# All attention heads as float32 products on row and column halves of TensorE, with w_val and w_out kept in SBUF

## The chip, the cores and the metric

The kernel runs on one core of a Trainium2 chip. The core has TensorE (matrix products, PE in the profile), VectorE (DVE), ScalarE (ACT), GpSimd (POOL) and SyncE (SP), which work through their own queues in the order in which the program lists them, and 16 DMA engines that move data between HBM and SBUF. The metric is the time of one execution in microseconds (us); less is better.

## The reference

Three stages follow each other on float32 data: batch 4, 12 heads, 448 tokens, head size 64, so a model width of 768.

```python
def _attn_ref(q, k, v):
    scores = scale * np.matmul(q, k.transpose(0, 1, 3, 2)) - np.log(S)
    attn = 1.0 / (1.0 + np.exp(-scores))
    return np.matmul(attn, v)
...
def _moe_ref(x, w_val, conv_w, w_out):
    for k in range(K):                       # K = 5, causal, per channel
        gate_pre += conv_w[k][None, None, :] * xp[:, k:k + S, :]
    gate = 1.0 / (1.0 + np.exp(-gate_pre))
    val = x @ w_val
    return (gate * val @ w_out)
...
def _moe2_ref(x, w_tok1, w_tok2, w_ch1, w_ch2):
    h = np.maximum(xt @ w_tok1, 0.0) @ w_tok2
    u = x + h.transpose(0, 2, 1)
    h2 = np.maximum(u @ w_ch1, 0.0) @ w_ch2
    return (u + h2)
```

The weights arrive as float64, which the kernel reads as pairs of 32-bit words; q, k and v are float32.

## The kernel before, in words

**Number formats.** Nearly every product is made of float32r parts. A float32 value x is split into H (x rounded to 12 significant bits) and L = x - H; a product is then three passes (H by H, L by H, H by L), each one PE instruction of 448 columns. A weight is decoded on the chip: `decode` takes a raw tile of float64 words, `[128, 2*768]` int32, and makes H and L with six DVE operations (lines 97, 99, 100, 103, 107 and 108) and two ACT operations (98 and 106). Raw tiles have two buffers, so the load of a piece waits until the piece two before it is decoded to the end (line 108).

**Attention.** The 12 heads of a batch are taken as 6 pairs (24 pairs in all). `KINDS` says how a pair is multiplied. Pairs 0 to 7 are kind n: float32 products on full tiles for the scores (`scores`, line 269; k is padded with zeros so that the 128 rows of one head's k and zeros meet both heads' q), and for attention times values (`native_av`) one full product (line 334) and then 3 products into each column half of TensorE (line 338), first the three of one head, then the three of the other. Pair 8 has split scores and float32 values. Pairs 9 to 23 are kind x: 16 float32r products for the scores (line 275) and 14 for the values (line 322), for which ACT computes every sigmoid twice (line 258, one into float32, one into H) and DVE takes the differences (lines 296, 299, 300) and splits q, k and v.

**Dense layers.** `post_pair` turns the attention output of a pair into H and L (`xs`) and into a gate by a convolution (line 353, four DVE operations). `dense_steps(b)` lists the products of batch b: w_val (108 instructions), w_out (108), transposes, w_tok1, w_tok2; both w layers are line 395. The list is woven between the attention pairs of batch b + 1 by `weave`; the last batch's list runs alone. Decoded w_val and w_out are written to HBM (`wscr`, line 175) and read back per column group and per batch (`w_load`, line 366, 42 loads), except that batch 0 uses w_val where it was decoded.

**Channel layers.** For each batch and each of 12 groups `fc` of 128 hidden channels, `ch1` (line 593) and `ch2` (line 607) make 18 products each. The 12 pairs of weight pieces are decoded once (`dec_ch`), the first `CHAN_LEFT` = 5 of them into a pool that becomes free when attention ends, the other 7 into a pool that takes the place of the dense layers' tiles and must wait for them.

**Order.** The queue of each engine is fixed when the program is built, by a scheduler that follows data dependences and priorities. A queue does not overtake itself: what stands behind a waiting instruction on DVE, ACT or SP waits too.

Of the kernel before, what the change touches and what calls it, by code (L numbers as in the profile page):

```python
# [24 lines left out]


@with_exitstack
def tile_kernel(ctx, tc, qT, kT, v, w_val, conv_w, w_out, w_tok1, w_tok2, w_ch1, w_ch2, out):
    """Every float32 product is made of float32r parts: x = H + L with H = x rounded to 12
    significant bits and L = x - H, which has 12 as well, so H and L are exact operands of a  # L30
    single-pass matmul. The weights come as float64 words and are split on chip into the same
    two parts. Activations are kept feature-major ([feature, token]). The attention of batch b + 1
    runs beside the dense layers of batch b; the first pairs of heads, when the weights are still
    being split, are multiplied as float32 instead."""
    nc = tc.nc
# [19 lines left out]
    KIND = KINDS + "x" * (NPT - len(KINDS))  # L55
# [4 lines left out]
    wscr = dram.tile([2, KD, P, 2, KD, P], F32, name="wscr")  # L60
# [23 lines left out]
    # --- float64 words -> float32 parts. The high word's sign, exponent (rebased by 896) and top  # L84
    # 11 fraction bits make hi; the other 9 + 32 fraction bits, times 2^(exponent - 20), make lo.
# [41 lines left out]
    wv = {}  # L127

    def dec_conv(pool):
        n = KD * KW  # L130

        def go(raw):
            st = pool.tile([P, 2, DM], F32R, tag="st", bufs=1, name="cwHL")
            h, lo = st[:, 0, :n], st[:, 1, :n]
# [22 lines left out]
    def dec_w(pool, sel, kk):  # L157
        w = (w_val, w_out)[sel]

        def go(raw):  # L160
            if sel == 0 and kk >= 2:
                tag = VAL_TAGS[kk - 2]
                hl = [attn.tile([P, DM], F32R, tag=tag, bufs=2, name=f"wv{n}") for n in range(2)]
            else:
                if sel == 0:
                    st = wts.tile([P, 2, DM], F32R, tag="wst", bufs=3, name="wv")
                else:
                    st = pool.tile([P, 2, DM], F32R, tag="st", bufs=1, name="st")
                hl = [st[:, n] for n in range(2)]
            if sel == 0:  # L170
                wv[kk] = hl
# [12 lines left out]
        return ld, go  # L184

    # ------------------------------------------------------------------ attention
    raw_t, hl_t, a_t = {}, {}, {}
    x_t, xs_t, gate_t = {}, {}, {}

    def load_qk(i):  # L190
# [508 lines left out]
```

## Time and profile before

| | |
|---|---|
| median of 3 runs | 817.37 us (816.83 to 820.62) |
| span of the profiled execution | 821.3 us, 0.5% above that median; the page gives no other time of this execution |
| PE matmul | busy 795.0 us, 97% of the span, 3712 instructions |
| PE weight loads | 677.8 us, 83% |
| DVE | 499.5 us, 61% |
| ACT | 389.4 us, 47% |
| DMA | 119.79 MB, mean 146 GB/s |

The busy time of PE is the sum of overlapping matmuls, so 97% is not a measure of how well PE works; the starts of its instructions are. A float32r product of 448 columns and a float32 product of 448 columns are not the same work: the profile counts two PE instructions for one float32 product. The page cuts the span into 40 slices of 20.5 us.

### The profile page before, as it was taken

What the parts mean: (1) busy time and instruction counts of PE and PEld (TensorE: products, weight loads), DVE (VectorE), ACT (ScalarE), POOL (GpSimd) and SP (SyncE); (2) the same over time, 40 slices, a digit from 0 to 9 for tenths busy, and PEclk for the clock granted to TensorE, in tenths of its full rate; (3) what the DMA queues carried; (4) which work ended last, traced back from release to release, by engine and by line L of the source; (5) the groups of instructions that cost most, each with busy time, mean ns of one, the idle gap of its engine ahead of it and who ended that gap; (6) DMA issues with size and microseconds to landing.
All of it is one profiled execution on the core that took longest, in us unless ns stands there. A gap on an engine that the chain in (4) does not pass through costs nothing.

```text
span 821.3 us, 10042 instructions
## 1 busy us (share of the span) xinstructions
PE 795.0 (97%) x3712; PEld 677.8 (83%) x3712; DVE 499.5 (61%) x818; ACT 389.4 (47%) x564; POOL 24.1 (3%) x83
## 2 busy tenths in 40 slices
PE   8899899999999999999998999999999999999998
PEld 3333487789998899988887899999999999999997
DVE  5877587789978899797768999962002200030002
ACT  6575465889788888897334444430002100020000
POOL 3221110000000000000000000000000000000000
PEclk9999989999999999999999999999999999999999
DMA  7898767564774547523687455424001400050001
GB/s 236 259 275 251 199 199 232 172 192 121 238 224 144 171 139 215 194 78 111 228 329 236 154 186 184 160 94 146 1 1 40 162 1 1 1 166 24 1 1 67
DMA packets 77855, 119.79 MB, mean 146 GB/s; under 512 B 7648, under 2 KB 68976, under 8 KB 77808
## 3 DMA queue, kind: packets, MB, share of 16 engines
q1 hardware_dynamic: 75984, 110.09, 42.5%
q0 software_dynamic: 1824, 9.08, 3.4%
q8 instruction: 29, 0.48, 0.2%
q14 instruction: 18, 0.15, 0.1%
HBM read 98.70 MB, written 20.45 MB: 145 GB/s over the span
## 4 chain that ended last, share of the span: by engine, by line
PE 77%; DMA 8%; DVE 6%; issue 5%; ACT 2%; POOL 1%; SPq 0%; POOLq 0%; DVEq 0%; ACTq 0%
PE psh L593 21%; PE pso L607 21%; PE psd L395 17%; PE pss L275 5%; PE psy L322 4%; PE pst L449 3%; DMA wscr<-st 3%; PE pst L436 3%; DMA raw<-w_tok 2%; DVE acc L353 1%; DMA raw<-w_ch 1%; DMA raw<-w_val 1%; PE pst L419 1%; DMA raw<-w_out 1%; DVE st L108 1%
## 5 line engine op out<-in xcount | busy, mean ns | idle before, releaser
L607 PE MATMUL pso<-r,wch 128*128 128x448 f32 x864 | 185.2, 366 | 0.0
L593 PE MATMUL psh<-us,wch 128*128 128x448 f32 x864 | 183.7, 366 | 0.0
L593 PEld LDWEIGHTS psh<-us,wch 128*128 128x128 f32 x864 | 162.3, 188 | 13.8
L607 PEld LDWEIGHTS pso<-r,wch 128*128 128x128 f32 x864 | 162.1, 188 | 13.7
L78 DVE SCALAR_TENSOR_TENSOR r<-psh,r 128x448 fp32r<-128x448 f32 x48 | 29.9, 623 | 215.7 <-ACT r L76 215.6
L76 ACT ACTIVATE r<-psh 128x448 fp32r<-128x448 f32 x48 | 26.0, 543 | 232.3 <-PE psh L593 232.0
L395 PE MATMUL psd<-gv,wst 128*128 128x448 f32 x432 | 98.0, 373 | 2.5 <-ACT x2T L410 2.4
L395 PEld LDWEIGHTS psd<-gv,wst 128*128 128x128 f32 x432 | 81.7, 191 | 11.3 <-ACT x2T L410 3.5
L395 PE MATMUL psd<-xs,wst 128*128 128x448 f32 x324 | 70.1, 366 | 0.0
L353 DVE SCALAR_TENSOR_TENSOR acc<-x,cw,acc 128x448 f32<-128x448 f32 x96 | 65.3, 681 | 0.8
L258 ACT ACTIVATE a<-pss,bias_s 128x896 f32<-128x896 f32 x60 | 60.4, 1007 | 10.2 <-PE pss L275 8.9
L395 PEld LDWEIGHTS psd<-xs,wst 128*128 128x128 f32 x324 | 60.9, 188 | 5.0
L98 ACT ACTIVATE dec_a<-dec_a,exp_b 128x768 int32<-128x768 int32 (+3 forms) x43 | 37.4, 869 | 53.9 <-DVE dec_a L97 51.3
L258 ACT ACTIVATE aH<-pss,bias_s 128x896 fp32r<-128x896 f32 x60 | 60.4, 1007 | 0.0
L269 PE MATMUL pss<-qn,kn 128*128 128x448 f32 x112 | 48.9, 578 | 11.5 <-POOL ident masks.py:199 4.0
L269 PEld LDWEIGHTS pss<-qn,kn 128*128 128x128 f32 x112 | 20.7, 198 | 36.9 <-issue 21.4
L275 PE MATMUL pss<-qH,kHL 128*128 128x448 f32 x128 | 47.5, 371 | 0.1
L275 PE MATMUL pss<-qL,kHL 128*128 128x448 f32 x128 | 46.7, 365 | 0.0
L322 PE MATMUL psy<-aH,vHL 128*128 128x448 f32 x120 | 39.3, 368 | 0.0
L103 DVE SCALAR_TENSOR_TENSOR dec_a<-raw,dec_a 128x768 int32<-128x768 int32 (+2 forms) x42 | 37.2, 887 | 3.2 <-ACT dec_a L98 3.1
L258 ACT ACTIVATE an<-pss,bias_s 128x896 f32<-128x896 f32 (+2 forms) x38 | 33.0, 881 | 10.9 <-PE pss L269 10.5
L100 DVE SCALAR_TENSOR_TENSOR dec_c<-raw,dec_c 128x768 f32<-128x768 uint32 (+2 forms) x42 | 37.3, 889 | 0.8
(93 smaller groups left out, 997.9 us busy)
## 6 DMA issues: line engine op xcount, KB each, us to landing
wst<-wscr SPq DMA_DIRECT2D x42, 768.0 KB, 4.7
raw<-w_ch SPq DMA_DIRECT2D x24, 768.0 KB, 4.4
rq<-qT SPq DMA_DIRECT2D x32, 224.0 KB, 4.7
rk<-kT SPq DMA_DIRECT2D x32, 224.0 KB, 3.8
uscr<-x2T SPq DMA_DIRECT2D x24, 224.0 KB, 3.0
u<-uscr SPq DMA_DIRECT2D x24, 224.0 KB, 4.2
ur<-uscr SPq DMA_DIRECT2D x24, 224.0 KB, 3.3
out<-ur SPq DMA_DIRECT2D x24, 224.0 KB, 2.2
```

Source lines behind the costliest of these rows:

```text
L78: nc.vector.scalar_tensor_tensor(out=l_out, in0=src, scalar=0.0, in1=f(h_out), op0=ALU.max, op1=ALU.subtract)
L98: nc.scalar.activation(out=a, in_=a, func=AF.Relu, scale=8.0, bias=exp_b)
L100: nc.vector.scalar_tensor_tensor(out=c.bitcast(F32), in0=lo.bitcast(U32), scalar=2.0**-32, in1=c, op0=ALU.mult, op1=ALU.add)
L103: nc.vector.scalar_tensor_tensor(out=a, in0=hi, scalar=-0x80000000, in1=a, op0=ALU.bitwise_and, op1=ALU.bitwise_or)
L258: nc.scalar.activation(out=out, in_=ps, func=AF.Sigmoid, bias=bias_s[rows], scale=QK_SCALE)
L269: nc.tensor.matmul(ps[:, cc, :S], k[:, at : at + P], q, start=True, stop=True)
L275: nc.tensor.matmul(ps[:, cc, :S], kHL[:, j, c * P : (c + 1) * P], mv[:, j, :], start=n == 0, stop=n == 1)
L322: nc.tensor.matmul(y[:, :S], lhsT, m, start=n == 0, stop=n == len(mv) - 1)
L353: nc.vector.scalar_tensor_tensor(out=acc, in0=x[:, t : t + S], scalar=cw[:, p * KW + t : p * KW + t + 1], in1=acc, op0=ALU.mult, op1=ALU.add,)
L395: nc.tensor.matmul(ps[:, :S], w(a, kk), s[:, c, :], start=kk == 0 and n == 0, stop=kk == KD - 1 and n == 2,)
L593: nc.tensor.matmul(ps[:, :S], wch[fc][:, 0, a, kk * P : (kk + 1) * P], us_t[b, kk][:, c, :], start=kk == 0 and n == 0, stop=kk == KD - 1 a ...
L607: nc.tensor.matmul(acc[j][:, :S], wch[fc][:, 1, a, j * P : (j + 1) * P], r[:, c, :], start=fc == 0 and n == 0, stop=fc == KF - 1 and n == 2,)
```

## The change

All 24 pairs are multiplied as float32. A score product now takes the 64 rows of one head: head 0 on rows 0 to 63 of TensorE, head 1 on rows 64 to 127, each into its own PSUM bank, 8 products in a pair. A value product takes all 128 rows and 64 columns: head 0 in columns 0 to 63, head 1 in columns 64 to 127, alternating, 8 products in a pair. There is one sigmoid for both heads of a chunk of 128 keys, and no split of q, k, v or of the attention weights. Decoded w_val lives in a pool `wval` on the left until the last batch has used it, decoded w_out in `wts`; `wscr`, its stores and its loads are gone. The pool for the first channel weights is opened only after w_val is released, and holds 3 groups in place of 5. `DEC_AT` says how many weight pieces are decoded beside each pair.

```diff
-KINDS = "nnnnnnnns"
-VAL_TAGS = ("qH", "qL", "kHL", "vHL")
-CHAN_LEFT = 5
+CHAN_LEFT = 3
+A_BUFS = 4
...
+DEC_AT = (1, 2, 2, 2, 2, 2, 2, 1, 1, 1, 1, 1)
...
-    wscr = dram.tile([2, KD, P, 2, KD, P], F32, name="wscr")
...
+    wval = tc.alloc_tile_pool(name="wval", bufs=1, side="left")
     attn = tc.alloc_tile_pool(name="attn", bufs=1, side="left")
...
+    wres = [
+        [[pool.tile([P, DM], F32R, name=f"w{sel}_{kk}_{n}") for n in range(2)] for kk in range(KD)]
+        for sel, pool in enumerate((wval, wts))
+    ]
...
-            decode(pool, DM, raw, hl[0], hl[1])
-            with tc.high_priority(0 if sel else -10):
-                for n in range(2):
-                    nc.sync.dma_start(
-                        wscr[sel, :, :, n, kk, :].rearrange("j p m -> p j m"),
-                        f(hl[n][:]).rearrange("p (j m) -> p j m", m=P),
-                    )
...
-        return ld, go
+        return ld, lambda raw: decode(pool, DM, raw, *wres[sel][kk])
...
+    def load_pair(i):
+        b, p = divmod(i, NP)
+        h0 = 2 * p
+        q = attn.tile([P, S], F32, tag="q", bufs=2, name="q")
+        k = attn.tile([P, S], F32, tag="k", bufs=2, name="k")
+        t = attn.tile([P, NF + 1, P], F32, tag="v", bufs=2, name="v")
+        nc.sync.dma_start(q, qT[b, h0 : h0 + 2].rearrange("h d s -> (h d) s"))
+        nc.sync.dma_start(k, kT[b, h0 : h0 + 2].rearrange("h d s -> (h d) s"))
...
+    def scores(i, c):
+        q, k, _ = raw_t[i]
         ps = psa.tile([P, 2, 512], F32, tag="s", bufs=2, name="pss")
+        at = KLAST if c == NF else c * P
+        for j in range(2):
+            rows = slice(j * D, (j + 1) * D)
+            nc.tensor.matmul(ps[:, j, :S], k[rows, at : at + P], q[rows], start=True, stop=True)
+        a = attn.tile([P, 2, S], F32, tag="a", bufs=A_BUFS, name="a")
+        nc.scalar.activation(out=a, in_=ps[:, :, :S], func=AF.Sigmoid, bias=bias_s, scale=QK_SCALE)
+        a_t[i, c] = a
+
+    def av(i):
+        vn = raw_t.pop(i)[2]
         y = psa.tile([P, 512], F32, tag="y", bufs=2, name="psy")
+        for c in range(NF + 1):
+            a = a_t.pop((i, c))
+            for j in range(2):
                 cols = slice(j * D, (j + 1) * D)
+                nc.tensor.matmul(y[cols, :S], vn[:, c, cols], a[:, j], start=c == 0, stop=c == NF)
+        x = attn.tile([P, PAD + S], F32, tag="x", bufs=2, name="x")
+        nc.gpsimd.memset(x[:, :PAD], 0.0)
+        nc.scalar.activation(out=x[:, PAD:], in_=y[:, :S], func=AF.Copy)
+        x_t[i] = x
...
-    def w_load(b, sel, j):
-        st = wts.tile([P, 2, KD, P], F32R, tag="wst", bufs=3, name="wst")
-        nc.sync.dma_start(f(st[:]), wscr[sel, j])
-        w_t[b, sel, j] = st
...
-                if held:
-                    return wv[kk][a][:, j * P : (j + 1) * P]
-                return w_t[b, sel, j][:, a, kk, :]
+                return wres[sel][kk][a][:, j * P : (j + 1) * P]
...
+        av(i)
+        if i + 1 < NPT:
+            scores(i + 1, 0)
+            scores(i + 1, 1)
+        if i + 2 < NPT:
+            load_pair(i + 2)
+        for _ in range(DEC_AT[i] if i < len(DEC_AT) else 0):
+            dec_go()
+        weave((base + 0.5) / NP * fast)
+        if i + 1 < NPT:
+            scores(i + 1, 2)
+            scores(i + 1, 3)
+        post_pair(i)
+        weave((base + 1.0) / NP * fast)
...
-    pso = tc.alloc_tile_pool(name="pso", bufs=1, space=bass.MemoryType.PSUM)
-    left = tc.alloc_tile_pool(name="p2l", bufs=1, side="left")
-    dec2 = tc.alloc_tile_pool(name="dec2", bufs=1, side="left")
...
     for fn in [fn for n, fn in tail] + rest[:nval]:
         fn()
+    wval.release()
+    pso = tc.alloc_tile_pool(name="pso", bufs=1, space=bass.MemoryType.PSUM)
+    left = tc.alloc_tile_pool(name="p2l", bufs=1, side="left")
+    dec2 = tc.alloc_tile_pool(name="dec2", bufs=1, side="left")
```

The change also moves instructions in the queues. On PE, beside the dense layers of batch 0, the queue before holds only full-tile products (line 395 dense, 322 values, 275 scores):

```order
L395 MATMUL psd<-gv,wst 128x448 x6
L322 MATMUL psy<-aL_1289,vHL 128x448
L322 MATMUL psy<-aH,vHL 128x448
L322 MATMUL psy<-aL_1313,vHL 128x448
L322 MATMUL psy<-aH,vHL 128x448
L395 MATMUL psd<-gv,wst 128x448 x6
L275 MATMUL pss<-qH,kHL 128x448
L275 MATMUL pss<-qL,kHL 128x448
L275 MATMUL pss<-qH,kHL 128x448
L275 MATMUL pss<-qL,kHL 128x448
L395 MATMUL psd<-gv,wst 128x448 x6
```

Of the change, at about the same place in the program (line 206 values on column halves, 194 scores on row halves, 267, 284 and 297 dense layers on full tiles):

```order
L267 MATMUL pst<-ident,x2T 128x128 x4
L206 MATMUL psy<-a,v 64x448
L297 MATMUL pst_1318<-wt2H,h_1149 128x448 x2
L297 MATMUL pst_1318<-wt2L,h_1149 128x448
L297 MATMUL pst_1318<-wt2H,h_1164 128x448 x2
L297 MATMUL pst_1318<-wt2L,h_1164 128x448
L267 MATMUL pst<-ident,x2T 128x128 x4
L206 MATMUL psy<-a,v 64x448 x7
L194 MATMUL pss<-q,k 128x448 x4
L284 MATMUL pst_1365<-x_1210,wt1H 128x384
```

PE now goes from one form of product to another (full tile, column halves, row halves) five times in these rows; in the whole queue it does so 121 times, against 28 times before, and 95 of the 121 come behind the first column group of w_out of batch 0.

On DVE, at the start of the program, where the first dense products are read out of PSUM (line 405 `gate`, then `gv`), the queue before has the gates of w_val ahead of most of the w_tok1 pieces (128x256):

```order
L97 TENSOR_SCALAR dec_a<-raw 128x256
L108 SCALAR_TENSOR_TENSOR st<-dec_c,raw 128x768
L405 TENSOR_TENSOR gate<-psd,gate 128x448
L99 TENSOR_SCALAR dec_c<-raw 128x256
L103 SCALAR_TENSOR_TENSOR dec_a<-raw,dec_a 128x256
L100 SCALAR_TENSOR_TENSOR dec_c<-raw,dec_c 128x256
L405 TENSOR_TENSOR gate<-psd,gate 128x448
L107 TENSOR_SCALAR raw<-dec_a 128x256
L82 TENSOR_TENSOR gv<-gate,gv 128x448
```

In the change the last three gates of w_val (line 253) stand behind the last w_tok1 piece and among the two w_tok2 pieces (128x448); these are the fourth and the fifth:

```order
L108 SCALAR_TENSOR_TENSOR wt1L<-dec_c,raw 128x256
L253 TENSOR_TENSOR gate<-psd,gate 128x448
L97 TENSOR_SCALAR dec_a<-raw 128x448
L99 TENSOR_SCALAR dec_c<-raw 128x448
L82 TENSOR_TENSOR gv<-gate,gv 128x448
L100 SCALAR_TENSOR_TENSOR dec_c<-raw,dec_c 128x448
L103 SCALAR_TENSOR_TENSOR dec_a<-raw,dec_a 128x448
L107 TENSOR_SCALAR raw<-dec_a 128x448
L97 TENSOR_SCALAR dec_a<-raw 128x448
L108 SCALAR_TENSOR_TENSOR wt2L<-dec_c,raw 128x448
L253 TENSOR_TENSOR gate<-psd,gate 128x448
```

So the reading of the last w_val groups now follows the loads of the last weight pieces.

On DVE again, where the dense layers of the last batch end (the last three `x2T` are line 453 before) and the channel layers begin, the queue before has its ninth channel piece finished (line 108) ahead of the last three `x2T`:

```order
L108 SCALAR_TENSOR_TENSOR wch<-dec_c,raw 128x768
L453 TENSOR_TENSOR x2T<-pst_4397,x2T 128x448
L99 TENSOR_SCALAR dec_c<-raw 128x768
L453 TENSOR_TENSOR x2T<-pst_4406,x2T 128x448
L100 SCALAR_TENSOR_TENSOR dec_c<-raw,dec_c 128x768
L453 TENSOR_TENSOR x2T<-pst_4415,x2T 128x448
```

In the change (line 301) it is the seventh piece that comes behind the last `x2T`:

```order
L301 TENSOR_TENSOR x2T<-pst_3433,x2T 128x448
L301 TENSOR_TENSOR x2T<-pst_3442,x2T 128x448
L301 TENSOR_TENSOR x2T<-pst_3451,x2T 128x448
L108 SCALAR_TENSOR_TENSOR wch<-dec_c,raw 128x768
L99 TENSOR_SCALAR dec_c<-raw 128x768
L78 SCALAR_TENSOR_TENSOR r<-psh,r 128x448
L100 SCALAR_TENSOR_TENSOR dec_c<-raw,dec_c 128x768
```

Where 9 of the 24 channel pieces were finished at this point, 6 are now.

## Rows read from the trace of the kernel before

**Rows 1.** The page, part 2: busy tenths of each engine in 40 slices.

```profile
PE   8899899999999999999998999999999999999998
...
DVE  5877587789978899797768999962002200030002
```

**Rows 2.** Busy time by stretch: us, PE, PEld, DVE, ACT, POOL, PEclk, DMA share, GB/s.

```profile
9.40:47.40 38.00, 34.05 (x99) 14.95 (x98) 31.94 (x46) 25.16 (x34) 6.58 (x18) 1.00 0.91 269
47.40:104.00 56.60, 49.85 (x139) 21.36 (x137) 37.17 (x59) 31.91 (x46) 7.84 (x22) 0.96 0.80 231
250.00:300.00 50.00, 49.19 (x252) 44.19 (x251) 45.17 (x74) 44.22 (x64) 0.30 (x3) 1.00 0.47 144
450.00:500.00 50.00, 50.00 (x249) 44.66 (x248) 47.90 (x76) 21.89 (x30) 0.00 (x0) 1.00 0.53 175
```

**Rows 3.** Timeline of PE: start, us to the last end, line, tile, form, count.

```profile
21.24 3.28 PE L338 MATMUL psy<-an,rv 128*64 128x448 f32 x12
24.45 2.40 PE L395 MATMUL psd<-xs,wv 128*128 128x448 f32 x10
...
64.78 2.47 PE L338 MATMUL psy<-an,rv 128*64 128x448 f32 x6
67.18 1.77 PE L269 MATMUL pss<-qn,kn 128*128 128x448 f32 x4
...
74.63 3.27 PE L269 MATMUL pss<-qn,kn 128*128 128x448 f32 x8
77.83 2.47 PE L338 MATMUL psy<-an,rv 128*64 128x448 f32 x6
...
88.96 3.17 PE L269 MATMUL pss<-qn,kn 128*128 128x448 f32 x8
91.96 0.92 PE L334 MATMUL psy<-an,rv 128*128 128x448 f32 x2
...
121.52 5.11 PE L395 MATMUL psd<-gv,wst 128*128 128x448 f32 x24
...
396.64 22.19 PE L395 MATMUL psd<-xs,wst 128*128 128x448 f32 x108
418.68 7.59 PE L395 MATMUL psd<-gv,wst 128*128 128x448 f32 x36
```

**Rows 4.** Line 108 up to 140 us: its tiles, durations, starts, and who waited.

```profile
L108 DVE SCALAR_TENSOR_TENSOR wv<-dec_c,raw x6: 947/958/960, 14.7 to 46.5; 128x768 fp32r<-128x768 f32 x6
L108 DVE SCALAR_TENSOR_TENSOR st<-dec_c,raw x6: 951/959/993, 58.6 to 102.9; 128x768 fp32r<-128x768 f32 x6
...
L108 DVE SCALAR_TENSOR_TENSOR wt1L<-dec_c,raw x4: 416/416/419, 106.5 to 122.3; 128x256 fp32r<-128x256 f32 x4
L108 DVE SCALAR_TENSOR_TENSOR wt2L<-dec_c,raw x2: 624/625/626, 131.8 to 134.4; 128x448 fp32r<-128x448 f32 x2
...
  DMA wscr<-st: 5.6, 2
```

**Rows 5.** Groups on DVE: busy us, mean ns, idle time before, what ended it.

```profile
L353 DVE SCALAR_TENSOR_TENSOR acc<-x,cw,acc 128x448 f32<-128x448 f32 x96 | 65.3, 681 | 0.8
...
L405 DVE TENSOR_TENSOR gate<-psd,gate 128x448 f32<-128x448 f32 x24 | 14.9, 620 | 1.2 <-PE psd L395 0.9
```

**Rows 6.** Timeline, DVE and PE, where the last channel pieces are decoded and used.

```profile
472.60 7.59 PE L593 MATMUL psh<-us,wch 128*128 128x448 f32 x36
...
534.00 0.55 DVE L97 TENSOR_SCALAR dec_a<-raw 128x768 int32<-128x768 int32 x1
...
537.51 0.96 DVE L108 SCALAR_TENSOR_TENSOR wch<-dec_c,raw 128x768 fp32r<-128x768 f32 x1
538.39 0.55 DVE L97 TENSOR_SCALAR dec_a<-raw 128x768 int32<-128x768 int32 x1
...
542.71 3.84 PE L593 MATMUL psh<-us,wch 128*128 128x448 f32 x18
```

**Rows 7.** DMA issues: engine, count, KB each, median us to landing.

```profile
raw<-w_val POOLq DMA_DIRECT2D x3, 768.0 KB, 7.3
```

More of the change, by code (lines that the diff above doesn't have):

```diff
@@ L54, in tile_kernel @@
     NPT = B * NP
[L55 removed]
+    KLAST = S - P
     assert D == 64 and REM == 64 and NF == 3
@@ L132, in go @@
         def go(raw):
-            st = pool.tile([P, 2, DM], F32R, tag="st", bufs=1, name="cwHL")
-            h, lo = st[:, 0, :n], st[:, 1, :n]
+            h = attn.tile([P, n], F32R, tag="acc", bufs=2, name="cwH")
+            lo = attn.tile([P, n], F32R, tag="acc", bufs=2, name="cwL")
             decode(pool, n, raw, h, lo)
@@ L202, in load_v @@
-    def load_v(i, diag):
-        b, p = divmod(i, NP)
-        t = attn.tile([P, NF + 1, 2 * D], F32, tag="rawv", bufs=2, name="rv")
-        vs = v[b, :, 2 * p * D : 2 * (p + 1) * D]
-        nc.sync.dma_start(t[:, :NF], vs[:R0].rearrange("(c p) x -> p c x", p=P))
-        for r in range(2):
-            rows, cols = slice(r * REM, (r + 1) * REM), slice(r * D, (r + 1) * D)
-            if diag:
-                nc.gpsimd.memset(t[rows, NF, (1 - r) * D : (2 - r) * D], 0.0)
-                nc.sync.dma_start(t[rows, NF, cols], vs[R0:, cols])
-            else:
-                nc.sync.dma_start(t[rows, NF], vs[R0:])
-        return t
@@ L330, in native_av @@
-    def native_av(i):
-        vn = raw_t.pop(i)[2]
-        a = [[a_t.pop((i, j, part)) for part in range(2)] for j in range(2)]
-        y = psa.tile([P, 512], F32, tag="y", bufs=2, name="psy")
-        nc.tensor.matmul(y[:, :S], vn[:, NF], a[0][1][:, 1], start=True, stop=False)
-        for j in range(2):
-            for c in range(NF):
-                cols = slice(j * D, (j + 1) * D)
-                nc.tensor.matmul(
-                    y[cols, :S], vn[:, c, cols], a[j][c // 2][:, c % 2], start=False, stop=c == NF - 1
-                )
-        nc.scalar.activation(out=new_x(i)[:, PAD:], in_=y[:, :S], func=AF.Copy)
+        nc.sync.dma_start(k, kT[b, h0 : h0 + 2].rearrange("h d s -> (h d) s"))
@@ L359, in post_pair @@
         gate_t[i] = gate
-    w_t = {}
-    def w_load(b, sel, j):
-        st = wts.tile([P, 2, KD, P], F32R, tag="wst", bufs=3, name="wst")
-        nc.sync.dma_start(f(st[:]), wscr[sel, j])
-        w_t[b, sel, j] = st
     def dense_steps(b):
-        units = [(b, sel, j) for sel in range(1 if b == 0 else 0, 2) for j in range(KD)]
         gv, x2T, x2, h1 = {}, {}, {}, {}
@@ L374, in proj @@
         def proj(sel, j, part):
-            held = b == 0 and sel == 0
             if part == 0:
-                u = -1 if held else units.index((b, sel, j))
-                if u == 0:
-                    for k in units[:2]:
-                        if k not in w_t:
-                            w_load(*k)
-                if not held and u + 2 < len(units):
-                    w_load(*units[u + 2])
                 cur["ps"] = psd.tile([P, 512], F32, tag="d", bufs=2, name="psd")
@@ L400, in proj @@
                 return
-            if not held:
-                del w_t[b, sel, j]
             if sel == 0:
@@ L483, in tile_kernel, with dec_load @@
     raws = []
-    def dec_load(first=False):
+    def dec_load():
         if decs:
             ld, go = decs.pop(0)
-            if first:
-                raw = wts.tile([P, 2 * DC], I32, tag="wst", bufs=3, name="raw")
-                ld(raw)
-            else:
-                raw = fetch(dec, ld)
-            raws.append((raw, go))
+            raws.append((fetch(dec, ld), go))
     def dec_go():
@@ L501, in tile_kernel @@
     load_pair(0)
-    dec_load(True)
     dec_load()
-    prep_pair(0)
-    craw = attn.tile([P, 2 * KD * KW], I32, tag="tmp", bufs=3, name="craw")
+    load_pair(1)
+    dec_load()
+    craw = attn.tile([P, 2 * KD * KW], I32, tag="craw", bufs=1, name="craw")
     ld, go = dec_conv(dec)
@@ L524, in late @@
         dn["late"] = tc.alloc_tile_pool(name="late", bufs=1, side="right")
-    scores(0, 0)
-    scores(0, 1)
-    for g in range(NH):
-        b, base = divmod(g, HB)
+    for c in range(NF + 1):
+        scores(0, c)
+    for i in range(NPT):
+        b, base = divmod(i, NP)
         fast = 0.95 if b == B - 1 else 1.0
@@ L537, in tile_kernel @@
             emitted = 0
-        if g % 2 == 0 and g // 2 + 1 < NPT:
-            load_pair(g // 2 + 1)
-            prep_pair(g // 2 + 1)
-        dec_go()
-        if g + 1 < NH:
-            scores(g + 1, 0)
-        weave((base + 0.33) / HB * fast)
-        if g + 1 < NH:
-            scores(g + 1, 1)
-        weave((base + 0.67) / HB * fast)
-        av(g)
-        if g % 2 == 1:
-            post_pair(g // 2)
-        weave((base + 1.0) / HB * fast)
+        av(i)
[12 more added lines that the diff above has]
+        weave((base + 1.0) / NP * fast)
     tail = pend
```

138 lines of the change are left out of this document (7 added, 131 removed).

## The prediction

> **What bounds the kernel now.** I read the slices of the page first. TensorE (PE) is at 80 or 90% and more in every slice, while VectorE (DVE) falls from the eighties and nineties to almost nothing over the last third [rows 1]. The stretches say the same with numbers: PE is busy 49.19 of 50 us from 250 and 50.00 of 50 from 450, but only 34.05 of 38 and 49.85 of 56.6 in the first 104 us [rows 2]. So PE bounds the middle and the end, and something else has a say at the start. Since busy time on PE is a sum of overlapping records, I took prices from starts in the timeline [rows 3]: 108 float32r products start within 418.68 - 396.64 = 22.04 us, so one costs 0.204 us. Eight float32 records take 91.96 - 88.96 = 3.00 us, so one costs 0.375 and a float32 product, which is two records, 0.75.
>
> DVE at the start does the decoding. One piece of 768 columns takes 538.39 - 534.00 = 4.39 us from the first operation to the first of the next [rows 6]. Line 108, its last operation, is 0.96 us there, 0.416 for w_tok1 and 0.625 for w_tok2 [rows 4], so I scale those pieces to 1.9 and 2.86 us.
>
> **What column halves and changes of form cost.** Three products into each column half, 12 records, take 24.45 - 21.24 = 3.21 us where 12 records in a row would take 4.5: the halves do run at once [rows 3]. The six records of one head alone take 67.18 - 64.78 = 2.40, which is 0.15 over 6 x 0.375. Eight score records followed by another form take 77.83 - 74.63 = 3.20, which is 0.20 over 3.00 [rows 3]. So going from one form to another costs 0.15 to 0.20 us, and it adds to the product time. I take 0.15 for the 21 changes into column halves and 0.20 for the other 74 behind the first column group of w_out; going into row halves stands in no row, and 0.20 is the nearer of the two since it, too, exposes a weight load. The bounds are 0 and 0.20.
>
> **The price of a pair.** A pair of kind x is 30 x 0.204 = 6.1 us now. After the change, 8 score products on row halves and 8 value products on column halves cost 8 x 0.375 = 3.0 each if both halves run at once: 6.0 us. No product on 64 rows stands in this trace. The column halves are the nearest row and overlap, so I take full overlap; the bounds are none (6.0 for the scores) and full (3.0).
>
> **Term A, the start.** I cut the program where the first column group of w_out of batch 0 ends: now at 121.52 + 18 x 0.204 = 125.2 us [rows 3], with the values of pair 7 still to do. The changed queue reaches the same place with the values of pair 7 and half of the scores of pair 8 done. PE has some 79 us of products and changes up to there (8 pairs at 6.5 with their changes, half a pair's scores 1.5, 108 x 0.204 = 22 and 18 x 0.204 = 3.7), so I asked DVE. It has 12 pieces x 4.39 = 52.7, four of w_tok1 7.6, two of w_tok2 5.7 (the gates of the last w_val groups now stand behind these), and 12 gates or `gv` at 0.62 less 0.08 overlap [rows 5] 6.4. The 0.08 is what line 108 overlaps the next decode: 0.96 long, 0.88 to the next start [rows 6]. Eight `post_pair` have four convolution operations of 0.681 each [rows 5], 0.60 by the same overlap, and one subtraction like a gate, 2.94 in all, so 23.5. The sum is 95.9 us from 9.4. If DVE never waited the cut would come at 105. It was busy 31.94 of 38 us in the first stretch, 84%, and 37.17 of 56.6, 66%, in the second [rows 2]. The waits of the second stretch include those on the `wscr` stores of `st`, 5.6 us in the row of line 108 [rows 4], which the change removes. What remains is the loads: a raw tile takes 7.3 us from issue to landing on POOL's queue [rows 7] against 4.39 of decoding, with two buffers. I take 90%: 9.4 + 95.9/0.9 = 116, so A = -9. The bounds are 100% (-20) and 84% (-2).
>
> **Term B, attention behind the cut.** Before: the values of pair 7 at 0.75 + 3.2 = 4.0, pair 8 with 16 x 0.204 = 3.3 and again 4.0, and 15 pairs at 6.1 = 91.8, together 103.1. After: half of the scores and the values of pair 8, 4.5, and 15 x 6.0 = 90, together 94.5; and the changes of form, 21 x 0.15 + 74 x 0.20 = 17.9, so 112.4. B = +9.3. What the change saves on products (8.6 us) is less than what it pays for the changes, because the dense products woven between are on full tiles. The bounds are -8.6 with changes that cost nothing, and those of the rivals below.
>
> **Term C, the channel layers.** When the dense layers of the last batch end (472.60 is the first double `ch1` [rows 6]), 9 of the 24 weight pieces are decoded now; afterwards 6 are, because the pool waits for w_val and holds three groups, and the rest for the dense tiles. Three decodes are 13.2 us. DVE has nearly no slack there, 47.90 of 50 us [rows 2]. The last piece is now ready at 538.39 and its products start at 542.71 [rows 6], so 4.3 us of the 13.2 are covered and 8.9 are not: PE would wait for `wch` in the last groups of batch 0. C = +9. It is 13 or 14 if what covers is gone, and 3 if DVE, with less work ahead, begins sooner or needs less than its share of a group.
>
> **Term D, waits in the middle.** PE is idle 0.81 of 50 us with DVE at 90% and ACT at 88% [rows 2], some 4.5 us over 275. The differences and second sigmoids go, so I take half back: D = -2 (0 to -4).
>
> **At nothing.** The stores and loads of `wscr` and the new long-lived tiles: the DMA engines were 47% busy in the middle [rows 2] and PE did not wait for loads there. In the first 47 us their share is 0.91, and that is in A. The new score loads are smaller than the old ones.
>
> **Sum.** 821.3 - 9 + 9.3 + 9 - 2 = 828.6 us of span. The median is 817.37 for a profiled span of 821.3, a factor 0.9952: 824 us. A difference under 0.5%, 813.3 to 821.5, is one that the measurement can't tell from no change.
>
> **The rivals.**
>
> *Changes of form are hidden* (faster). If the next form's weights load while the last product of the old form still streams, the 17.9 us are not paid, B is -8.6 and the span 810.7: 807 us. Against it stand the 2.40 and 3.20 us [rows 3], but they come from places with one change each, and none into row halves. It decides when a change costs less than 0.07 us: 95 x (0.19 - 0.07) = 11 us turn 824 into 813. At half price it is 815. TensorEngine Tiling (Array Packing) of the Trainium skill, section Key Properties, says that a change of tiling mode drains TensorE, which speaks against this rival; the trace agrees with 0.15 and 0.20 us.
>
> *DVE never waits at the start.* With no stores to wait for, loads could keep ahead. A is -20 rather than -9: 813.5, and 809 with the lower end of C. For it: 5.6 us of the waits are gone. Against it: two raw buffers, and 7.3 us to a load. It holds from a DVE share of 95% on.
>
> *Row halves overlap only in part.* If each of four chunks in a pair exposes one weight load, at the 0.20 us of a change into full form, 15.5 pairs cost 12.4 us more: 841 of span, 837 us. TensorE: Matmul & The Clock Gate of the Trainium skill, Part 3, measured 3.07 times for four row tiles, not four; by that ratio scores would cost 1.3 times 3.0, an estimate of +14 us and 838. No run here shows it yet.
>
> *Row halves do not overlap at all*, so that the change doesn't do what it says. Scores cost 6.0, 15.5 x 3.0 = 46.5 us more behind the cut, and nothing at the start, where 79 + 24 us of PE still fit under DVE's 107: 875 of span, 871 us. For it speaks only that no row has 64-row products; against it that the column halves overlap.
>
> **How the numbers follow.** The forecast as summed has 0.48, with 811 to 837 as its own range from the ends of A, C and D. Hidden changes have 0.18, DVE without waits 0.16, partial overlap 0.10 and none 0.08. The range 806 to 839 leaves out the last and the tails of the others. Faster: 0.15 from hidden changes, 0.07 from the start, 0.03 from my own range, 0.25. Same: 0.12 of my own, 0.09 of the start, 0.03 of changes at half price, 0.24. Slower: 0.33 of my own, 0.10 and 0.08 of the two overlap cases, 0.51.
>
> **What the profile after would show.** Eight score records of two heads starting in 1.5 us, in pairs at nearly one time, or in 3.0 if rows do not overlap. Between the last record of one form and the first of another, 0.15 to 0.20 us over 0.375 or 0.204. The first w_out group of batch 0 starting at about 112 us, with DVE at some 90% until then. `ch1` of the last groups of batch 0 waiting on DVE for `wch`, 9 us in all. In the middle, PE without idle time but for the changes. The forecast is wrong if the changes cost under 0.07 us, if DVE's share at the start is near 100% or near 80%, or if `ch1` never waits.

## The result and the profile after

The change makes the kernel slower: 827.61 us median (824.15 to 829.17) against 817.37, a ratio of 1.0105 with a 95% interval of 1.0075 to 1.0135. The profiled execution has a span of 827.1 us against 821.3. Executions in which the granted clock fell for a long time are left out of every ratio, and the profile of e4 below (clock 0.656, 1099.4 us) is one of them, so its stages are not known. I cut both traces at the two places where the prediction cut its sum: the end of the first column group of w_out of batch 0, and the start of the last product of the dense layers of the last batch.

| us from the trace | before | after | difference | predicted |
|---|---|---|---|---|
| start, up to the cut | 125.2 | 112.7 | -12.5 | A -9 |
| from the cut to the end of the dense layers | 347.2 | 357.3 | +10.1 | B +9.3, D -2 |
| channel layers and the end | 348.9 | 357.1 | +8.2 | C +9 |
| span | 821.3 | 827.1 | +5.8 | +7.3 |

Of the first 18 products of `ch2`, all lie before the second place in the kernel before and 13 in the change. So 1.0 us of products moved across it: like for like the middle is 11.1 us longer and the channel layers 7.2.

The slices of VectorE on the page show where work went. They answer to [rows 1]:

```profile
DVE  5898844243433434234589399993002200030002
```

After the first slice VectorE is still at eight and nine tenths up to 100 us, falls to two to four tenths through the middle, and is full in slices 24 to 27, where the channel pieces are decoded. The busy times by stretch answer to [rows 2] (us, PE, PEld, DVE, ACT, POOL, granted clock, DMA share, GB/s):

```profile
9.40:47.40 38.00, 29.63 (x123) 9.45 (x121) 35.37 (x54) 30.69 (x41) 6.05 (x12) 0.91 0.57 198
47.40:104.00 56.60, 50.62 (x215) 28.10 (x217) 50.19 (x94) 38.84 (x57) 8.21 (x18) 0.91 0.47 150
...
250.00:300.00 50.00, 48.72 (x234) 31.98 (x235) 20.09 (x35) 20.48 (x31) 0.90 (x6) 1.00 0.19 60
```

From 9.4 to 104 VectorE is busy (35.37 + 50.19) / 94.6 = 90% of the time. From 250 to 300 its load has more than halved, from 45.17 to 20.09 us, and TensorE is no busier for it: 48.72 where it was 49.19 [rows 2].

The timeline of TensorE from the cut on (line 194 is scores on row halves, 206 values on column halves, 245, 284 and 297 dense, 267 transposes; the last four rows, with `ch1` in line 431 and `ch2` in 445, are from the channel layers) answers to [rows 3]:

```profile
108.45 5.66 PE L245 MATMUL psd<-gv,w 128*128 128x448 f32 x24
...
149.91 3.23 PE L206 MATMUL psy<-a,v 128*64 128x448 f32 x16
153.07 1.77 PE L194 MATMUL pss<-q,k 64*128 64x448 f32 x8
154.78 0.67 PE L297 MATMUL pst<-wt2H,h 128*128 128x448 f32 x2
...
161.12 1.77 PE L194 MATMUL pss<-q,k 64*128 64x448 f32 x8
162.82 1.49 PE L245 MATMUL psd<-gv,w 128*128 128x448 f32 x6
164.15 0.60 PE L267 MATMUL pst<-ident,x2T 128*128 128x128 f32 x4
164.68 0.97 PE L206 MATMUL psy<-a,v 128*64 128x448 f32 x2
165.57 0.67 PE L297 MATMUL pst<-wt2H,h 128*128 128x448 f32 x2
...
166.89 0.60 PE L267 MATMUL pst<-ident,x2T 128*128 128x128 f32 x4
167.42 3.22 PE L206 MATMUL psy<-a,v 128*64 128x448 f32 x14
170.57 1.77 PE L194 MATMUL pss<-q,k 64*128 64x448 f32 x8
172.28 0.44 PE L284 MATMUL pst<-x,wt1H 128*128 128x384 f32 x1
...
181.56 0.36 PE L297 MATMUL pst<-wt2L,h 128*128 128x448 f32 x1
181.85 3.23 PE L206 MATMUL psy<-a,v 128*64 128x448 f32 x16
185.00 1.77 PE L194 MATMUL pss<-q,k 64*128 64x448 f32 x8
...
512.58 0.47 PE L431 MATMUL psh<-us,wch 128*128 128x448 f32 x1 [0.59 <-ACT wch L106]
...
541.49 0.47 PE L431 MATMUL psh<-us,wch 128*128 128x448 f32 x1 [0.41 <-ACT wch L106]
542.20 3.72 PE L431 MATMUL psh<-us,wch 128*128 128x448 f32 x17 [0.24 <-DVE wch L108]
546.55 3.93 PE L445 MATMUL pso<-r,wch 128*128 128x448 f32 x18 [0.63 <-ACT r L76]
```

Three things stand in the rows up to 185 us. Eight score records of two heads take 162.82 - 161.12 = 1.70 us: 1.50 for four in a row in each half, both halves at once, and 0.20 for the change of form. Sixteen value records take 185.00 - 181.85 = 3.15, which is 3.00 and 0.15. And where the scheduler put the first value product of a pair alone (164.68, the products of the other seven at 167.42), it has no partner in the other half: 0.89 us for two records, and the fourteen still take 3.15, so the pair pays 0.89 more than in one piece. Four of the 16 pairs behind the cut are split like this, one of them into three.

The table of waits (us in all, times, longest us), in this order: TensorE from the cut to 470 us, TensorE in the channel layers of batch 0 (470 to 560), VectorE up to 115 us:

```profile
PE pst L284 <- ACT x L269: 2.7, 3, 1.3
PE psd L245 <- ACT x2T L258: 2.2, 2, 2.0
PE psd L245 <- DVE x2T L301: 1.0, 1, 1.0
...
PE psh L431 <- ACT wch L106: 1.7, 4, 0.6
PE pso L445 <- ACT r L76: 1.3, 2, 0.6
PE psh L431 <- DVE wch L108: 0.7, 2, 0.4
...
DVE dec_a L97 <- DMA raw<-w_val: 5.4, 3, 3.0
DVE dec_a L97 <- DMA craw<-conv_w: 4.8, 1, 4.8
DVE dec_a L97 <- DMA raw<-w_tok: 3.6, 3, 2.1
DVE dec_a L97 <- DMA raw<-w_out: 2.2, 2, 1.5
```

In the middle TensorE waits for copies of transposes and for the reading of PSUM. In the same channel layers the kernel before has no wait on TensorE at all; here decoding comes late piece after piece (the last four rows of the timeline), which costs by many small waits, not by one long one. At the start VectorE waits for almost nothing but raw weights.

### The profile page after: what moved, and what is told of

The parts are those of the page before. It is cut to its first block, busy times and chain, and to the rows that moved or that the text cites. A ratio compares the mean times of both kernels' runs of the same rounds, so it can differ in the third digit from the quotient of the medians.

```text
span 827.1 us, 9458 instructions
## 1 busy us (share of the span) xinstructions
PE 793.3 (96%) x3776; PEld 612.5 (74%) x3776; DVE 376.0 (45%) x635; ACT 295.7 (36%) x440; POOL 20.7 (2%) x73
## 4 chain that ended last, share of the span: by engine, by line
PE 73%; DVE 16%; DMA 7%; ACT 2%; issue 1%; SPq 0%; POOL 0%; POOLq 0%; DVEq 0%; ACTq 0%
PE psh L431 17%; PE psd L245 17%; PE pso L445 17%; PE psy L206 7%; PE pss L194 6%; PE pst L284 4%; PE pst L297 3%; DMA raw<-w_ch 2%; DVE dec_a L103 2%; DVE acc L221 2%; DVE dec_c L100 2%; DMA raw<-w_val 2%; DVE wch L108 1%; DVE dec_a L97 1%; DVE raw L107 1%; DMA raw<-w_tok 1%
## 5 line engine op out<-in xcount | busy, mean ns | idle before, releaser
L194 PE MATMUL pss<-q,k 64*128 64x448 f32 x384 | 95.4, 602 | 15.4 <-ACT a L196 11.3
L245 PE MATMUL psd<-gv,w 128*128 128x448 f32 x432 | 97.7, 376 | 3.4 <-ACT x2T L258 2.2
L196 ACT ACTIVATE a<-pss,bias_s 128x896 f32<-128x896 f32 x96 | 92.5, 999 | 22.7 <-PE pss L194 22.6
L245 PEld LDWEIGHTS psd<-gv,w 128*128 128x128 f32 x432 | 80.3, 191 | 23.1 <-issue 7.9
L245 PE MATMUL psd<-xs,w 128*128 128x448 f32 x432 | 92.1, 369 | 2.0 <-DVE gate L253 1.0
L245 PEld LDWEIGHTS psd<-xs,w 128*128 128x128 f32 x432 | 80.0, 188 | 18.2 <-issue 6.5
L206 PE MATMUL psy<-a,v 128*64 128x448 f32 x384 | 85.4, 565 | 0.9 <-ACT a L196 0.8
L194 PEld LDWEIGHTS pss<-q,k 64*128 64x128 f32 x384 | 34.5, 195 | 62.1 <-issue 35.8
L206 PEld LDWEIGHTS psy<-a,v 128*64 128x64 f32 x384 | 26.7, 142 | 49.7 <-issue 48.0
L284 PE MATMUL pst<-x,wt1H 128*128 128x384 f32 x112 | 31.1, 347 | 2.9 <-ACT x L269 2.7
```

The lines of the kernel that those rows point to most:

```text
L194: nc.tensor.matmul(ps[:, j, :S], k[rows, at : at + P], q[rows], start=True, stop=True)
L196: nc.scalar.activation(out=a, in_=ps[:, :, :S], func=AF.Sigmoid, bias=bias_s, scale=QK_SCALE)
L206: nc.tensor.matmul(y[cols, :S], vn[:, c, cols], a[:, j], start=c == 0, stop=c == NF)
L245: nc.tensor.matmul(ps[:, :S], w(a, kk), s[:, c, :], start=kk == 0 and n == 0, stop=kk == KD - 1 and n == 2,)
L284: nc.tensor.matmul(ps[:, :HALF], a, x[:, m], start=n == 0, stop=n == len(mm) - 1)
```

## The experiments

My theory: TensorE pays for each change of form, so it matters how often it goes from one to another; the start is paced by VectorE and by the raw weights that it waits for; the channel layers lose what three late decodes cost. The rivals: the middle pays by product (a weight load exposed at each 64-row or 64-column product), work on VectorE and ScalarE alone sets the start, and the channel layers are longer for another reason. Every kernel ran beside the kernel before, whose median was 820.09, 819.65 and 818.46 us in the three series. The times by stage are from the traces.

| kernel | ratio to before (95%) | cut | cut to end of dense | channel | span |
|---|---|---|---|---|---|
| after | 1.0105 (1.0075 to 1.0135) | 112.7 | 357.3 | 357.1 | 827.1 |
| e1 grouped | 1.0130 (1.0091 to 1.0169) | 114.9 | 361.0 | 355.1 | 830.9 |
| e2 split | 1.0137 (1.0104 to 1.0170) | 109.3 | 363.6 | 356.6 | 829.5 |
| e3 fewer decodes | 1.0039 (1.0012 to 1.0067) | 111.4 | 358.0 | 352.2 | 821.7 |
| e4 three raw tiles | 1.0036 (1.0011 to 1.0062) | | | | |
| e5 early pool | 1.0147 (1.0116 to 1.0178) | 122.1 | 354.6 | 350.4 | 827.1 |
| e6 staging tile | 1.0194 (1.0167 to 1.0221) | 118.2 | 357.3 | 355.5 | 831.0 |
| e7 = e5 and e4 | 0.9994 (0.9977 to 1.0012) | 109.6 | 354.5 | 352.0 | 816.1 |
| e8 = e7, bank, order, grouped | 0.9826 (0.9802 to 0.9851) | 107.7 | 345.0 | 349.9 | 802.6 |
| e9 = e8 not grouped | 0.9876 (0.9835 to 0.9917) | 109.0 | 345.3 | 349.9 | 804.1 |
| e10 = e5, stores later | 1.0027 (0.9999 to 1.0055) | 111.2 | 355.0 | 350.6 | 816.8 |
| e11 = e8, stores later | 0.9815 (0.9769 to 0.9861) | 107.6 | 344.6 | 349.9 | 802.1 |
| e12 = before, three raw tiles | 0.9910 (0.9878 to 0.9942) | 117.2 | 343.0 | 348.9 | 809.1 |

Each row of stages is one execution. Kernels with the same start (after, e3) differ by 1.3 us at the cut, those with the same middle (after, e3, e6) by 0.7, and those with the same channel layers (after, e1, e2, e6) by 2 us, so stages are known to about that.

### e1 and e2: fewer and more changes of form

In e1, `pe[0]` is the product that was put on PE last and `GROUP_AT` is 8, so from pair 8 on these pieces keep their order in the queue:

```diff
+        after = lambda: tc.issue_after(pe[0].ins) if i >= GROUP_AT else nullcontext()
...
-        av(i)
+        with after():
+            scores(i, 2)
+            scores(i, 3)
+        with after():
+            av(i)
         if i + 1 < NPT:
+            with after():
                 scores(i + 1, 0)
                 scores(i + 1, 1)
...
-        if i + 1 < NPT:
-            scores(i + 1, 2)
-            scores(i + 1, 3)
```

> The changed kernel, but from pair 8 on the last two score chunks of a pair, its values and the first two score chunks of the next pair follow each other on PE without dense products between them: 63 changes of form behind the first column group of w_out of batch 0 instead of 95. If a change of form costs 0.2 us, 32 fewer give 6.4 us back, less about 1.5 us in which the values wait for the last sigmoid: some 5 us faster than the changed kernel, span 822. If what the changed kernel loses in the middle is a cost of each 64-row or 64-column product, the time stays: 827.

e2 puts dense products between any two chunks:

```diff
             scores(i + 1, 0)
+            weave((base + 0.25) / NP * fast)
             scores(i + 1, 1)
...
             scores(i + 1, 2)
+            weave((base + 0.75) / NP * fast)
             scores(i + 1, 3)
```

> The changed kernel, but with dense products woven between any two score chunks: 145 changes of form behind the first column group of w_out instead of 95. If a change costs 0.2 us, 50 more cost 10 us: span 837. If the cost goes by product, or if the next weights are loaded under cover, nothing: 827.

Both middle stages came out longer, 361.0 and 363.6 against 357.3: e1 against both forecasts. The whole times do not tell the two from the changed kernel (the intervals overlap), so what follows rests on the stages. To see why, I summed the starts of all TensorE records from the cut to the end of the dense layers against their price in the undisturbed places (0.2035 us per float32r record of 448 columns, 0.1735 of 384, 0.109 a transpose, 0.369/2 a record on a half whose partner runs).

| us over that price | after | e1 | e2 | e9 |
|---|---|---|---|---|
| scores on row halves | 10.6 | 7.1 | 15.4 | 8.0 |
| values on column halves | 7.0 | 3.3 | 3.3 | 3.3 |
| transposes | 5.8 | 14.8 | 6.8 | 0.7 |
| dense and w_tok | 14.4 | 16.3 | 18.6 | 12.7 |
| of all these: single waits over 0.35 us | 8.8 | 19.0 | 9.3 | 4.2 |

In e1 scores and values give back 3.5 + 3.7 = 7.2 us, the 3.7 because no pair is split any more. Outside the waits the whole falls from 29.0 to 22.5 us, 6.5 for 32 changes fewer, as forecast. But the waits grew by 10.2. The waits of e1 on TensorE from 112 to 476 us, against those of after above (its lines 248, 261 and 287 are 245, 258 and 284 of after):

```profile
PE psd L248 <- ACT x2T L261: 5.3, 7, 3.0
PE pst L287 <- ACT x L272: 5.0, 5, 2.2
PE pst L300 <- ACT x2T L261: 1.7, 4, 1.0
```

One of them, in its timeline:

```profile
248.24 0.60 PE L270 MATMUL pst<-ident,x2T 128*128 128x128 f32 x4
249.53 0.44 PE L287 MATMUL pst<-x,wt1H 128*128 128x384 f32 x1 [0.69 <-ACT x L272]
```

Four transposes are followed at once by the product that needs ScalarE's copy of them. In the changed kernel the same step had value and score products in between (166.89 transposes, 167.42 values, 170.57 scores, 172.28 w_tok1), which cost changes of form and hid the copy. So the changes of form were partly paid for by the waits that they covered.

In e2 the trace has 143 changes where the changed kernel has 95. The four split pairs are whole again, which takes away 10 changes worth 3.7 us; the 58 new ones come to 9.5 us outside the waits (6.3 more in all, 0.5 of it in waits, and the 3.7), 0.16 each where 0.2 was forecast. That the start of e2 is 3.4 us earlier was not followed up; by it the span hides half of what the middle lost. The products are the same in all three kernels, so a cost by product cannot make these differences.

### e3: is it the decoding that lengthens the channel layers?

```diff
-        for fc in range(CHAN_LEFT, KF):
+        for fc in range(CHAN_LEFT, KF - 3):
             dec_ch(fc)
+        for fc in range(KF - 3, KF):
+            wch[fc] = wch[KF - 4]
```

> The changed kernel, but the last three channel groups use the decoded weights of the ninth, so six of the 24 channel pieces are never loaded or decoded (the output is not the reference's). If PE waits in the channel layers of batch 0 because three decodes come late, those layers take some 7 us less: span 820. If the channel layers are longer for another reason (the end of the program, a lower clock), nothing: 827.

The channel layers took 352.2 us, 4.9 less where 7 was forecast, with one wait of TensorE left (455 to 560 us):

```profile
PE psh L431 <- DVE wch L108: 0.4, 1, 0.4
```

It is the decoding, for most of the difference: 4.0 of the 4.9 us lie between products of the channel layers, 0.9 behind the last product of the program. Of the remaining 3.3 us over the kernel before, 1.0 are the five `ch2` products that lie behind the cut here; the rest was not followed further.

### e4 and e12: do raw tiles pace the start?

```diff
-        raw = pool.tile([P, 2 * DC], I32, tag="raw", bufs=2, name="raw")
+        raw = pool.tile([P, 2 * DC], I32, tag="raw", bufs=3, name="raw")
...
     dec_load()
+    dec_load()
```

> The changed kernel with three raw tiles instead of two, so that weight loads run a piece further ahead at the start. If loads pace the decoding there (DVE waits 11 us for them before the first product of w_out), that product comes some 5 us earlier, at 103 instead of 108 us, and the span is 822. If DVE or ACT work alone sets the start, 827.

The ratio goes from 1.0105 to 1.0036, 0.7% or 5.6 us: VectorE waited 11.2 us (5.4 + 3.6 + 2.2) for raw pieces in the table above. Where the time was saved e4 itself does not show. The pair e5 and e7 below does: they differ by the raw tiles alone, the waits for raw pieces up to the cut are 20.5 and 6.4 us, and the cut comes at 122.1 and 109.6.

The same edit to the kernel before:

> The kernel before the change with three raw tiles. If loads of raw pieces pace its start as well, with its stores and reloads beside them, the first product of w_out comes some 5 us earlier (116 instead of 121) and the span is 816. If the staging tile of w_out and DVE work set its start, 821.

It is 0.9% faster than before, more than forecast: the cut comes at 117.2 instead of 125.2. But the waits for raw pieces fall only from 13.2 to 9.7 us there, and those in front of `st`, the tile through which w_out is stored, from 11.6 to 5.2. So that raw loads alone paced the kernel before is not shown. Why a third raw tile shortens the waits on `st`, and why 4 us are gained between the cut and the end of the dense layers, was not followed up.

### e5 and e10: an early pool, and what stores do to the start

```diff
-CHAN_LEFT = 3
+CHAN_LEFT = 5
...
-        for sel, pool in enumerate((wval, wts))
+        for sel, pool in enumerate((wval, wval))
...
+        if 10 <= i < 16:
+            w_store(0, i - 10)
+            w_store(1, i - 10)
...
     attn.release()
+    wval.release()
...
+    left = tc.alloc_tile_pool(name="p2l", bufs=1, side="left")
...
+                if b == B - 1:
+                    return w_t[sel, j][:, a, kk, :]
```

> The changed kernel, but w_val and w_out leave the chip when attention ends: they are also stored to HBM beside batches 1 and 2, batch 3 reads them back per column group, and the pool for the first channel weights opens at the end of attention (380 instead of 416 us) with 5 groups instead of 3. If the 8 us that the channel layers lost come from the late pool, they come back: the channel layers take 349 us as before the change, span 819. If they come from DVE being slower per piece, the ninth to twelfth groups still wait and the span stays at 826.

In this kernel `wval` holds both w_val and w_out. The channel layers came back to 350.4 us, within 1.5 us of before. The span didn't move, since the start was 9.4 us later. The scheduler had put the stores not beside batches 1 and 2 but where each piece was decoded, between 14 and 94 us. Its DMA issues up to 115 us (KB each, us to landing):

```profile
wscr<-w SPq DMA_DIRECT2D x24, 384.0 KB, 4.3
raw<-w_out POOLq DMA_DIRECT2D x6, 768.0 KB, 6.9
...
raw<-w_val POOLq DMA_DIRECT2D x3, 768.0 KB, 7.1
```

and those of the changed kernel up to 110 us:

```profile
raw<-w_out POOLq DMA_DIRECT2D x6, 768.0 KB, 4.8
...
raw<-w_val POOLq DMA_DIRECT2D x3, 768.0 KB, 5.0
```

That gave an experiment that I had not planned: VectorE has no wait on these stores, yet raw pieces take 2 us longer to land, and its waits for them up to the cut go from 11.2 to 20.5 us, which is all that the start lost. It is busy 30.90 us of the first stretch instead of 35.37:

```profile
9.40:47.40 38.00, 29.72 (x121) 9.96 (x121) 30.90 (x47) 27.16 (x36) 4.26 (x9) 0.87 0.90 272
```

e10 chains the same stores behind the loads of pairs 12 to 17:

```diff
+            with tc.issue_after(sp[0].ins):
                 w_store(0, i - 10)
                 w_store(1, i - 10)
```

> The early pool with two raw tiles, and the stores to HBM really behind the loads of pairs 12 to 17, after the start. If the stores between 14 and 94 us made the start of e5 9 us later by slowing the loads of raw pieces, the first product of w_out comes at 108 again and the channel layers stay at 350 us: span 818. If the start of e5 was late for another reason, 827.

The cut is at 111.2 again, the channel layers at 350.6, the span 816.8: the losses of e5 are those of the stores, and those of the changed kernel in the channel layers are those of the late, small pool (1.0 of the 6.5 us are the five `ch2` products, which lie before the cut again). Whether lateness or size costs more was not separated.

### e6: the staging tile

```diff
+            st = pool.tile([P, 2, DM], F32R, tag="st", bufs=1, name="st")
+            decode(pool, DM, raw, st[:, 0], st[:, 1])
+            for n in range(2):
+                nc.sync.dma_start(wscr[kk, n], f(st[:, n]))
+            for n in range(2):
+                nc.sync.dma_start(f(wres[sel][kk][n][:]), wscr[kk, n])
```

> The changed kernel, but each decoded piece of w_out goes through one staging tile to HBM and is read back into the resident tile, as a wait of the kernel before. If a good part of the earlier start comes from w_out no longer passing through a single staging tile, the first product of w_out comes some 8 us later (116 instead of 108) and the span is 834. If it comes from less work on DVE alone, 109 and 828.

The first product of w_out came at 114.0, 5.6 us later, between the two forecasts. VectorE never waited for the staging tile's stores; its waits for raw pieces of w_out rose from 2.2 to 7.7 us:

```profile
DVE dec_a L98 <- DMA raw<-w_out: 7.7, 4, 2.5
```

So here, too, it is the traffic that delays the raw pieces: those of w_out take 6.4 us to land instead of 4.8. In the kernel before, waits on `st` came on top, as term A below tells.

### e7, e8, e9 and e11: a faster version, and what made it so

e7 joins e5 and e4.

> The early pool with 5 groups and three raw tiles together: if start and channel layers are separate losses, 5 and 8 us add up: span 814, under the kernel before. If an earlier start is given back in the middle, 819.

The start is 3.1 us earlier than in the changed kernel in spite of the stores, the middle is that of e5 (354.5 and 354.6 us), so nothing is given back there, and the span of 816.1 lies between the forecasts. The ratio is 0.9994. e8 adds grouping from pair 8 on, as in e1, a PSUM bank for the transposes while attention runs (`y` has one buffer in place of two), and another order of steps:

```diff
-        y = psa.tile([P, 512], F32, tag="y", bufs=2, name="psy")
+        y = psa.tile([P, 512], F32, tag="y", bufs=1, name="psy")
...
+            if b < B - 1:
+                pt = psa.tile([P, NF + 1, P], F32, tag="t", bufs=1, name="pst")
...
-        ... + tr(2) + t1(0, 0) + t1(0, 1)
-        steps += pj(1, 4) + tr(3) + t2(0) + t2(1) + pj(1, 5) + tr(4) + t2(2) + tr(5)
+        ... + tr(2)
+        steps += pj(1, 4) + t1(0, 0) + t1(0, 1) + tr(3) + pj(1, 5) + t2(0) + tr(4) + t2(1) + tr(5) + t2(2)
```

> As the one before, with the score chunks and values of a pair together on PE (63 changes of form behind the first w_out group), the transposes in a PSUM bank of their own while attention runs, and w_tok1 behind another w_out group. If grouping failed only because the dense pieces then met their own waits (19 instead of 9 us), these are mostly gone and the 7 us of fewer changes show: span 807. If the waits stay, 818.

It is the first changed version whose interval lies wholly below 1, at 0.9826. e9 takes the grouping out again.

> The kernel of e8 without the grouping on PE: early pool, three raw tiles, transposes in a PSUM bank of their own, w_tok1 behind another w_out group. If the gain of e8 over e7 is the fewer changes of form (7 us in the middle) and the rest the shorter waits, this one lies at a span of 810 with R and C pieces as long as in the changed kernel. If the gain is the bank alone, 803.

The span is 804.1, so most of the gain of e8 over e7 (12.0 of 13.5 us by the spans, 1.2 of 1.7% by the ratios) is that of the bank and the order of steps, not of grouping; my expectation for e8 had the emphasis wrong. The sums above show where: transposes 0.7 over their price instead of some 4 in e7, and no split pair, 3.7, with 81 changes of form in place of 95. Grouping then takes 18 more changes away, but e8 has 7.0 us of long waits where e9 has 4.2, and the middle stays (345.0 and 345.3). The long waits on TensorE of e9, from 109 to 454 us, are short ones now:

```profile
PE psd L265 <- DMA wst<-wscr: 0.9, 2, 0.6
PE psd L265 <- ACT x2T L278: 0.6, 3, 0.2
PE pst L307 <- ACT x L292: 0.6, 1, 0.6
```

Which share is the bank's and which the order's was not separated.

> The kernel of e8 with its stores held back in the same way. If the DMA engines, busy all the time there from 9 to 47 us, still delay raw pieces with three tiles, the start comes some 3 us earlier: span 800. If three tiles cover it, 802.

e11 has the lowest time that I saw, 801.93 us against 818.46, a ratio of 0.9815, but it cannot be told from e8. With three raw tiles the stores no longer matter: raw pieces of w_out land in 7.4 us in e8 and 4.9 in e11, and the cuts are at 107.7 and 107.6.

## Why the prediction was right

It forecast 824 us, slower; 827.61 was measured. On the profiled executions the sum is closer, 828.6 against 827.1. The 3.6 us in the median come from the factor 0.9952: the span of before lay 0.5% above its median, that of after 0.1% below. The mechanisms of A, B and C were there, but that the sum is so near is partly luck: against the forecast the start came out 3.5 us shorter, the middle 2.8 longer and the channel layers 0.8 shorter.

**Term A** was -9 and measured -12.5. The share of VectorE, 90%, is what the trace shows (93.1 of 103.3 us from 9.4 to 112.7); I had chosen it between 84 and 100%, not worked it out, so that it fits is luck. Its work is 93.1 us where I had 95.9, and these 2.8 us, at 90%, are 3.1 of the 3.5 that the term was off. The cost that I named as removed, the waits on the `wscr` stores of `st`, is there, and larger than the 5.6 us that I read [rows 4]. The list of waits of the kernel before has one more, for which the profile names nothing that ended it:

```profile
DVE st L108 <- issue: 6.0, 1, 6.0
```

It ends at 96.25 us, when ScalarE's wait for the same tile ends, and that one is for the store:

```profile
96.24 0.84 ACT L106 ACTIVATE st<-dec_a 128x768 fp32r<-128x768 f32 x1 [8.16 <-DMA wscr<-st]
```

So 11.6 of the 18.3 us by which VectorE's waits up to the cut shrank (34.9 to 16.6) were on `st`; those for raw pieces fell only from 13.2 to 11.2. Yet it is the stores that have to go and not these waits alone: e5 has stores again, without a wait of VectorE on them, and gives back 9.4 of the 12.5 us by later raw pieces.

**Term B** was +9.3 and measured, with D, +10.1, or +11.1 like for like. Products give 8.7 us back; 1.0 of it are the five of `ch2`, so attention gives 7.7 (forecast 8.6). What lies over the prices of the table went from 18.8 to 37.7 us, 18.9 more (forecast 17.9 for the changes), but it is made differently. In these prices a stay on row halves costs 1.70 - 8 x 0.369/2 = 0.22 and one on column halves 3.15 - 16 x 0.369/2 = 0.20, close to what I took from [rows 3], but going out of full tiles only 0.29 - 0.204 = 0.09 (181.56 to 181.85), where I had put 0.15 or 0.20 on every change. With 34 stays on row halves, 16 pairs on column halves and 40 ways out of full tiles that is 34 x 0.22 + 16 x 0.20 + 40 x 0.09 = 14.3 us. Another 3.7 are the four split pairs, which the prediction did not have though the order of the queue shows one; 0.9 are not assigned. That a change costs, and costs by change, is shown by e2, with 0.16 us each. TensorEngine Tiling (Array Packing) of the Trainium skill, section Key Properties, has the drain at a change of mode. The trace agrees with 0.09 to 0.22 us by the form that is left.

**Term C** was +9 and measured +8.2, or +7.2 like for like. By their starts, the channel products lie 6.3 us further apart than before, nearly all of it in the first 90 us; 0.9 us stand behind the last product of the program. That the decoded pieces come late is shown by e3 and e10. Line 108 of the last piece starts at 558.2 us instead of 542.3: the piece of 537.51, ready at 538.39, that I called the last is the one before it, since the row at 538.39 begins another decode [rows 6]. My 4.3 us of cover hold for it, as it carries the `ch1` weights of the last group.

**Term D** failed: -2 was forecast and nothing came. The single waits over 0.35 us in the middle add to some 8.8 us before as after. TensorE was busy 270.66 us of the 275 from 125 to 400 before and 271.10 after, while VectorE went from 234.74 to 107.82. Most of TensorE's long waits there are for a chain (transposes, ScalarE's copy, the next product), and halving the load of the other engines did not shorten them; e9 did, to 4.2 us, by order and a bank.

**The rivals.** Hidden changes fell by the 1.70 and 3.15 us; VectorE without waits by its 90%; row halves that overlap in part or not at all by 1.70 us for eight records, against 3.00 one after the other. The full overlap that I had assumed for both kinds of halves was not in [rows 3]: 12 records in 3.21 us, one head's products queued behind the other's, overlap only in part. With the heads alternating it came. TensorE: Matmul & The Clock Gate of the Trainium skill, Part 3, has 3.07 for four row tiles. No run here has four; for two tiles of 64 rows the trace shows the full factor of two beside the price of the change.

## What to carry to other kernels

Counting products is not enough where TensorE is cut into halves: count how often it goes from one form to another in the queue as it is, and look for products that stand alone on a half. Before foreign work is taken out from between dependent steps, ask what it hid: fewer changes of form lost in e1, where dependent steps then waited for each other, and hardly paid in e8, where the transposes had a bank of their own and their consumers stood further off. And where a load paces the start, look at what moves beside it: stores that the waiting engine has no wait on cost 9.4 us here with two raw buffers, and nothing that could be measured with three. One more raw buffer alone made the kernel before 0.9% faster.

## What I had not expected of the hardware

Stores of 9.4 MB (24 of 384 KB) between 14 and 94 us made raw pieces of w_out land in 6.9 us instead of 4.8, with no wait of VectorE on the stores. The granted clock was 0.91 on average in both first stretches after the change, and 1.00 and 0.96 before [rows 2]. It was at the lower level, 1.2 GHz, for 17 us in four pieces, three of which begin 0.4 to 1.3 us after TensorE had stood still for some 2 us (another such gap, up to 28.1 us, has none behind it); before, for one piece of 10 us. As VectorE set the start, I did not separate what that costs.
